# Row sums moved behind the transposes, one PSUM bank for all dispatches, an earlier v cast, and spare products in the tail of a linear-attention and soft-MoE kernel

## The chip, the cores and the metric

The kernel runs on one core of a Trainium2 chip. The metric is the device time of one launch in microseconds. Five engines work side by side, each with its own queue of instructions that it takes in order: PE multiplies matrices (its weight loads are shown as a separate row, PEld), DVE and ACT work elementwise and read the results out of PSUM, POOL works elementwise on SBUF, SP starts transfers. POOL starts transfers too. An engine waits for another one on a semaphore.

## The reference, cut to what matters

```
state = zeros(B, H, D, D)                       # B=4, H=8, S=768, D=48
for t in range(S):
    cur   = (u * k_t) outer v_t
    y_t   = r_t @ (state + cur)
    state = w[:, None] * state + k_t outer v_t
x = y as (B*S, H*D) = (3072, 384)

logits = x @ phi                                # (3072, 32): 8 experts, 4 slots each
d = softmax of logits over the 3072 rows        # dispatch
slot_out[e] = relu((d.T @ x)[e] @ w1[e]) @ w2[e]   # w1: 8 x 384 x 1024, w2: 8 x 1024 x 384
c = softmax of logits over the 32 slots         # combine
out = c @ slot_out
```

The kernel never subtracts a maximum. It keeps exp(logits) once, as `Le` (rows of x on the partitions) and transposed as `LexpT` (slots on the partitions, 3072 columns). The dispatch sum and its normaliser come from `Le`. The combine step needs for each of the 3072 rows the sum of exp(logits) over the slots: these **row sums** are products of columns of `LexpT` with a vector of ones.

## The kernel before, in words

**The loop.** The 8 heads are taken as 4 pairs, so there are 16 units (4 batches by 4 pairs), index `m` or `mu`. A unit has two halves of 384 time steps (`g` = 0 and 1, three chunks of 128 each), so the loop has 32 steps `i` and five steps of run-in; step `i` is even for the first half of a unit and odd for the second. k and r are scaled by powers of w on POOL (`scale`), transposed on PE (`t_pe`: k into bank T0 in even steps, r into bank T1 in odd ones) and copied out by ACT (`t_evac`, tiles `kT` and `rT`). In odd steps k is transposed back (`b_pe`, into T0) and copied out by DVE (`b_evac`, tile `kn`). `v_cast` turns v into bf16 on ACT (tile `v_bf`), `v_pe` spreads it over the partitions, `v_evac` copies it out. `a_pe` makes the scores in bank Ab, `mask_f` masks them on DVE (tile `AT`, line L303). `m_pe` and `z_evac` make the states (`Z`, `dv`), `y_pe` puts the result together, `y_evac` copies it to `x`. `prod_f` on DVE multiplies r, straight from bank T1, by k.

All instructions stand in the order in which the code is written; nothing reorders them. The code is written as a software pipeline: step `i` holds `a_pe(i+1)`, `y_pe(i)`, `v_pe(i+2)`, `m_pe(i+1)`, the transposes of unit `mu+2` and, at its end, `v_cast(mu+2)` in odd steps. `v_pe` of the very next step is the first to read that cast.

**The routing inside the loop.** While batch `b+1` is computed, `route(i, part)` does the expert routing of batch `b`, spread over the 8 steps `s` = 0 to 7: `xt_mm` transposes a chunk of x and ACT copies it out (`xT`); one step later `lg_mm` makes its logits; after three chunks ACT takes the exponential (`le_ev`). At `s` = 4 and `s` = 7 a finished half batch is dispatched: `disp` (twelve products, lines L421 and L425), `disp_ev` (DVE adds the result to `acc`), and `le_t` and `let_ev` (the transpose into `LexpT`). The dispatch at `s` = 4 writes the end of bank T1 (`ds_e`), the one at `s` = 7 the end of bank T0 (`ds_o`). Both stand ahead of the step's transposes. A wait is for a whole bank's tile: a dispatch that writes the end of T1 waits until `prod_f` has read the front of T1, and `b_pe`, which writes T0, waits until `acc` has been taken out of T0. ACT and DVE also read one bank's tile one after the other, in the order of the code.

**The weights.** w1 and w2 are loaded by transfers that POOL starts (`load_w`), converting to bf16 on the way. The table `W_AT` says after which loop step how many of the 16 are started; w2 goes into the buffers of batches 1 and 2.

**The tail.** After the loop the last two half batches (6 and 7) go through transposes, logits, exponential and dispatch. Then 24 row-sum products with 96 columns of weights each (L539, for the rows of the first six half batches), the dispatch of half batch 7, the sums `uns` on DVE, the w1 products (L565: 48 products of 512 columns, four of them side by side in the array), relu on ACT and DVE, eight transposes per group (L577), two copies of the transposed hidden layer (`hT`: DVE L580, ACT L582), the w2 products (L588), 24 row-sum products with 32 columns (L599, the remaining rows) ahead of the last expert's share of w2, and at last 24 products `LexpT` by `so` (L620), scaled by DVE and ACT and written out in eight transfers. The weights of all row sums and of L620 are every 24th column of `LexpT`.

`keep_warm` (L139) multiplies a tile of zeros; it stands only at the start of the kernel.

Of the kernel before, what the change touches and what calls it, by code (L numbers as in the profile page):

```python
# [9 lines left out]
def kernel(  # L10
# [26 lines left out]
    T = L * C  # L37
    P2 = 2 * D
    nN = Nn // C
    nG = B * G  # L40
    nU = B * nQ
# [10 lines left out]
    def O(ins):  # L52
        return tc.keep_in_program_order(ins)
# [35 lines left out]
    ds_e = T1[:, 768:1024].bitcast(f32)[:, 0:NA]  # L89
    ds_o = T0[:, 768:1024].bitcast(f32)[:, 0:NA]  # L90


    LexpT = cst.tile([128, Nn], bf, name="LexpT")
# [43 lines left out]
    def keep_warm(n, cols=512):  # L137
        for _ in range(n):
            O(pe.matmul(Yb[:, 0:cols], warm[:, 0:128], warm[:, 0:cols], start=True, stop=True))  # L139


    s_i = cst.tile([128, J], i32, name="s_i")
# [293 lines left out]
    def route(i, part):  # L436
        b, s = divmod(i - LAG, 2 * nQ)
        if not 0 <= b < B - 1 or i == nH - 1:
            return
        ne = 2 * b  # L440
        ch = [(ne, c) for c in range(L)] + [(ne + 1, c) for c in range(L)]
        done = {L + 1: ne, 2 * L + 1: ne + 1}.get(s)
        if part == 0:
            if done is not None:
                ds = ds_o if s % 2 else ds_e
                disp(done, ds)
                disp_ev(done, ds)
                le_t(done)
# [17 lines left out]
    for i in range(-5, nH):  # L466
        mu, odd = divmod(i, 2)
        if 0 <= i + 1 < nH:
            a_pe(i + 1)
            mask_f(i + 1)  # L470
        if odd == 0 and 0 <= mu + 1 < nU:
            prod_f(mu + 1)
        if i == nH - 1:
            for c, (bank, eng) in enumerate(((Vb[:].bitcast(bf)[:, 0:Dm], act), (T1[:, 0:Dm], dve), (xT_p, act))):
                xt_mm(nG - 2, c, bank)
                xt_ev(nG - 2, c, bank, eng)
        if 0 <= i < nH:
# [42 lines left out]
    disp(n0 - 1, ds_o)  # L520
# [12 lines left out]
    le_ev(n0 + 1, LG1)  # L533
    lp = Mb[:].bitcast(bf)[:, 0:T]
    le_t(n0, lp)
    let_ev(n0, lp)
    nP = (nG - 2) * T // nN
    for i in range(nN):
        O(pe.matmul(Rs[0:nP, i:i + 1], LexpT[:, i:nP * nN:nN], ones[:, 0:1],  # L539
                    start=(i == 0), stop=(i == nN - 1), skip_group_check=True))  # L540
    disp(n0 + 1, ds_o, False)


    for g in range(2):
        def half(t):
            return t[:, 0:nM * ES].rearrange("p (m j x) -> p m j x", m=nM, j=EG)[:, :, :, g * Spe:(g + 1) * Spe]
        O(dve.tensor_add(uns[:, :, g, :, g * Spe:(g + 1) * Spe], half(acc), half(ds_o)))
    le_t(n0 + 1)
    let_ev(n0 + 1)
    csr = cst.tile([128, 1], f32, name="csr")  # L550
    O(dve.scalar_tensor_tensor(out=csr[:], in0=acc[:, NA - 1:NA], scalar=1e-9, in1=ds_o[:, NA - 1:NA],
                               op0=ALU.add, op1=ALU.add))
    O(dve.reciprocal(csr[:], csr[:]))

# [6 lines left out]
    for g in range(2):  # L561
        for a in range(2):
            for mi in range(nM):
                for j in range(EG):
                    O(pe.matmul(hb[g][a][32 * j:32 * j + 32, 0:FH], uns[:, mi, g, j, :],  # L565
                                w1_all[:, g * EG + j, mi, a * FH:(a + 1) * FH],
                                start=(mi == 0), stop=(mi == nM - 1), skip_group_check=True))
            src = hb[g][a][:, 0:FH].rearrange("p (q y) -> p y q", y=nF)
            dst = h_sb[g][:, :, a * PH:(a + 1) * PH]
            if a == 0:  # L570
                O(act.activation(out=dst, in_=src, func=AF.Relu))
            else:
                O(dve.tensor_scalar(out=dst, in0=src, scalar1=0.0, scalar2=None, op0=ALU.max))
    for g in range(2):
        bank = (T0, T1)[g]
        for y in range(nF):
            O(pe.transpose(bank[:, y * C:(y + 1) * C], h_sb[g][:, y, :], ident[:]))  # L577
        dst = hT[g].rearrange("p y c -> p (y c)")
# [16 lines left out]
    for y in range(nF):  # L595
        for j in range(EG - 1):
            w2_mm(1, j, y)
    for i in range(nN):
        O(pe.matmul(Rs[nP:128, i:i + 1], LexpT[:, nP * nN + i:Nn:nN], ones[:, 0:1],  # L599
                    start=(i == 0), stop=(i == nN - 1), skip_group_check=True))  # L600
    rsr = cst.tile([128, nN], f32, name="rsr")
    O(dve.reciprocal(rsr[:], Rs))
    for y in range(nF):
# [53 lines left out]
```

## Time and profile before

| | |
|---|---|
| Median of 3 runs | 136.2 us (134.25, 136.2, 137.34) |
| Profiled execution | 134.71 us, of which the span from first to last instruction is 132.9 us |
| Granted clock of PE, mean | 0.951 |
| Busy: PE / PEld / DVE / ACT / POOL | 107.2 / 85.2 / 98.8 / 84.8 / 60.6 us |
| Weight transfers started by POOL | 12.59 MB, last bytes at about 105 us |
| Loop | first mask at 13.5 us, last at 96.3 us |
| Tail up to the first output transfer | 98 to 119 us |
| Output transfers | 119 us to the end |

A line of the timeline reads: start, time, engine, line, operation, destination and sources, shape, how many were merged, and in brackets how long the engine had stood idle before and what ended that. In a row of the windows the columns are the stretch, its length, busy time and number of instructions of PE, PEld, DVE, ACT and POOL, the granted clock of PE as a share of full speed, the share of the transfer engines that was busy, and GB/s. In the groups the last columns are total and mean time of one instruction. In the table of waits they are the total, how often, and the longest.

### The profile page before, as it was taken

The page shows a single profiled execution, that of the slowest core. Times are in us where ns is not written, and L with a number is a line of the kernel's source. Part 1 is how long each engine was busy: PE and PEld are TensorE (multiplying, and loading weights), DVE is VectorE, ACT ScalarE, POOL GpSimd, SP SyncE. Part 2 cuts the span into 40 slices and gives each one's busy share as a digit, 9 for nine tenths or more (in the row PEclk, how much of TensorE's full clock was granted, in tenths as well). Part 3 has the DMA queues.
Part 4 walks back from the last instruction along what each step waited for, and adds up shares of the span by engine and source line. Part 5 has one row for each costly group of instructions (what it writes and reads, how often), then busy time and mean ns, then how long its engine had stood idle before and what let it go on. Part 6 is the DMA issues. An engine that isn't in the chain of part 4 may idle for free.

```text
span 132.9 us, 4372 instructions
## 1 busy us (share of the span) xinstructions
PE 107.2 (81%) x1806; PEld 85.2 (64%) x1806; DVE 98.8 (74%) x197; ACT 84.8 (64%) x177; POOL 60.6 (46%) x72
## 2 busy tenths in 40 slices
PE   6497858989888979889888898987999998989100
PEld 1255737767667867777777687785889836975000
DVE  2999999999999995979997898999760123059500
ACT  3559857778578768977895978888672124049400
POOL 5979999984459636766493792100000000000000
PEclk9999999999999999999999999999999559999955
DMA  2999999999999999999999999999999700009995
GB/s 80 298 356 374 374 363 306 359 375 339 368 380 341 218 220 214 179 195 190 216 211 202 216 165 188 211 214 221 216 209 210 126 2 5 0 5 364 407 416 233
DMA packets 21093, 31.79 MB, mean 239 GB/s; under 512 B 1361, under 2 KB 18258, under 8 KB 21074
## 3 DMA queue, kind: packets, MB, share of 16 engines
q0 software_dynamic: 2656, 12.59, 47.9%
q1 hardware_dynamic: 18418, 18.93, 41.4%
q8 instruction: 14, 0.23, 0.6%
q14 instruction: 5, 0.04, 0.1%
HBM read 39.38 MB, written 4.72 MB: 332 GB/s over the span
## 4 chain that ended last, share of the span: by engine, by line
PE 43%; DVE 28%; issue 9%; ACT 9%; POOL 3%; DVEq 1%; POOLq 0%; ACTq 0%
DVE AT L303 6%; PE Vb L283 6%; DVE prod L256 5%; DVE Z L342 5%; DVE dv L344 5%; PE Ab L539 4%; PE T L234 3%; PE Yb L367 3%; PE Mb L324 3%; ACT rT L240 2%; PE Ab L298 2%; ACT kT L240 2%; DVE W L181 2%; PE T L246 2%; ACT v_bf L269 2%
## 5 line engine op out<-in xcount | busy, mean ns | idle before, releaser
L227 POOL TENSOR_TENSOR kr<-raw,W 128x576 bf16<-128x576 f32 x30 | 43.2, 1453 | 18.0 <-PE T L234 15.4
L303 DVE TENSOR_TENSOR AT<-Ab,mask_ut 128x768 bf16<-128x768 f32 x32 | 30.3, 948 | 2.0 <-PE Ab L298 2.0
L283 PEld LDWEIGHTS <-Q 128*128 128x128 bf16 x288 | 15.6, 97 | 10.4 <-issue 9.8
L283 PE MATMUL Vb<-v_bf,Q 128*128 128x96 bf16 x288 | 17.4, 205 | 5.4 <-ACT v_bf L269 4.6
L240 ACT COPY kT<-T 128x768 bf16<-128x768 bf16 x16 | 12.8, 800 | 7.4 <-PE T L234 6.5
L234 PE MATMUL T<-ident,kr 128*128 128x128 bf16 x192 | 16.4, 225 | 0.0
L240 ACT COPY rT<-T 128x768 bf16<-128x768 bf16 x16 | 12.8, 800 | 4.8 <-PE T L234 3.4
L374 ACT CAST x<-Yb 128x288 bf16<-128x288 f32 x32 | 13.1, 409 | 3.7 <-PE Yb L367 3.6
L256 DVE TENSOR_TENSOR prod<-T,kT 128x768 bf16<-128x768 bf16 x16 | 15.1, 946 | 0.0
L289 ACT CAST vn<-Vb 128x288 bf16<-128x288 f32 x32 | 13.0, 408 | 2.1 <-ACT x L374 1.4
L344 DVE TENSOR_TENSOR dv<-vn,Mb 128x288 bf16<-128x288 bf16 x32 | 14.2, 442 | 0.0
L234 PEld LDWEIGHTS <-kr 128*128 128x128 bf16 x192 | 12.3, 100 | 0.6 <-issue 0.6
L298 PE MATMUL Ab<-rT,kT 64*128 64x128 bf16 x192 | 10.9, 219 | 1.2 <-DVE AT L303 1.1
L324 PE MATMUL Mb<-vn,kn 128*128 128x96 bf16 (+2 forms) x80 | 11.2, 238 | 0.0
L342 DVE TENSOR_TENSOR Z<-Mb,bmask 128x192 bf16<-128x192 f32 x32 | 11.1, 346 | 0.0
L251 DVE COPY kn<-T 128x768 bf16<-128x768 bf16 x16 | 8.9, 554 | 2.3 <-PE T L246 2.0
L365 PE MATMUL Yb<-Z,rT 128*128 128x96 bf16 x80 | 9.4, 203 | 1.2 <-DVE Z L342 1.0
L354 PE MATMUL Yb<-vn,AT 128*128 128x48 bf16 x192 | 10.3, 185 | 0.0
L269 ACT CAST v_bf<-raw 128x576 bf16<-128x576 f32 x15 | 10.1, 676 | 0.0
L367 PE MATMUL Yb<-dv,ident 128*128 128x288 bf16 x32 | 9.1, 283 | 1.1
L398 ACT COPY xT<-Xb 128x384 bf16<-128x384 bf16 x19 | 9.2, 485 | 0.2 <-PE Xb L389 0.2
L354 PEld LDWEIGHTS <-AT 128*128 128x128 bf16 x192 | 7.0, 96 | 3.2
(140 smaller groups left out, 214.4 us busy)
## 6 DMA issues: line engine op xcount, KB each, us to landing
w_all<-in_moe_w_dram POOLq DMA_DIRECT2D x8, 768.0 KB, 9.1
raw<-in_moe_w_dram POOLq DMA_DIRECT2D x7, 768.0 KB, 15.2
out_dram<-raw SPq DMA_DIRECT2D x4, 768.0 KB, 5.9
raw<-in_k_dram SPq DMA_DIRECT2D x8, 288.0 KB, 6.6
raw<-in_r_dram SPq DMA_DIRECT2D x8, 288.0 KB, 6.1
raw<-in_v_dram SPq DMA_DIRECT2D x8, 288.0 KB, 6.4
raw<-in_k_dram SPq DMA_DIRECT2D x2, 1152.0 KB, 10.3
raw<-in_r_dram SPq DMA_DIRECT2D x2, 1152.0 KB, 9.9
```

What stands on the lines that cost most here:

```text
L227: O(eng.tensor_mul(kr[:, j].rearrange("p j (h s) -> p j h s", s=64)[:, :, :, 0:D], src, W[j][:, q].rearrange("p j (h d) -> p j h d", h=2)))
L234: O(pe.transpose(bank[:, x * C:(x + 1) * C], kr[:, j, x, :], ident[:]))
L240: O(act.copy(t[:].rearrange("p (s j) -> p s j", j=J), bank[:, 0:S].rearrange("p (j s) -> p s j", j=J)))
L256: O(dve.tensor_mul(pr[:].rearrange("p (s j) -> p s j", j=J), T1[:, 0:S].rearrange("p (j s) -> p s j", j=J), st["kT", m][:].rearrange("p (s ...
L283: O(pe.matmul(Vb[:, c * P2:(c + 1) * P2], Q3[:, o:o + C], vb[:, :, g, j, :], start=(j == 0), stop=(j == JV - 1)))
L298: O(pe.matmul(Ab[:, e, c * C:(c + 1) * C], kT[s, t], rT[s, t]))
L303: O(dve.tensor_mul(AT[:], Ab[:, :, 0:T].rearrange("p e (c t) -> p e c t", c=L), mask_ut[:, None, None, :].to_broadcast([128, 2, L, C])))
L324: O(pe.matmul(o, kn[:, g * L + c, :], vc, start=first, stop=True, skip_group_check=True))
L342: O(dve.tensor_mul(Z[:], Mb[:, 0:2 * P2].rearrange("p (c e) -> p c e", c=2), bmask[:, None, :].to_broadcast([128, 2, P2])))
L344: O(dve.tensor_mul(dv[:], st["v", i][:].rearrange("p c e d -> p (c e) d"), Mb[:, 288:288 + 2 * L, None].to_broadcast([128, L * 2, D])))
L354: O(pe.matmul(Yb[:, o:o + D], AT[:, e, c, :], vn[:, c, e, :], start=first, stop=False, skip_group_check=True))
L374: O(act.copy(st["x", n][:, :, q * P2:(q + 1) * P2], Yb[:, 0:L * P2].rearrange("p (c e) -> p c e", c=L)))
```

## The change

Four things are done at once.

1. The row sums are made in one go with 128 columns of weights each (24 products instead of 24 of 96 and 24 of 32). The first eight stand between the transposes of the two groups, the other sixteen where L599 stood. The copy of the second `hT` is halved between DVE and ACT.
2. Every dispatch in the loop writes the end of T1 (`ds_p`), and it stands behind the step's `t_pe` (`route(i, 1)`). The logits and the x transposes stay ahead of it (`route(i, 0)`); the copies of ACT stay at the end (`route(i, 2)`).
3. `v_cast` stands in even steps, one step earlier. `W_AT` starts some weight transfers one step earlier.
4. In the tail five products of 512 columns (`busy`, on a tile of w1, into the second half of Ab, never read) stand between the routing steps.

```
+    def busy(n):
+        keep_warm(n, Ab[:, 1, :], w1_all[:, 0, 0, :])
...
     le_ev(n0, LG0)
+    busy(1)
     for c, (bank, eng) in enumerate(...):
         xt_mm(n0 + 1, c, bank)
         xt_ev(n0 + 1, c, bank, eng)
-    disp(n0, ds_o, False)
+    busy(1)
+    disp(n0, ds_t, False)
+    busy(1)
     for c in range(L):
         lg_mm(n0 + 1, c, LG1)
     le_ev(n0 + 1, LG1)
+    busy(1)
...
-    for i in range(nN):
-        O(pe.matmul(Rs[0:nP, i:i + 1], LexpT[:, i:nP * nN:nN], ones[:, 0:1], ...))
-    disp(n0 + 1, ds_o, False)
+    disp(n0 + 1, ds_t, False)
+    busy(1)
...
+    def row_sums(a, z):
+        for i in range(a, z):
+            O(pe.matmul(Rs[:, i:i + 1], LexpT[:, i:Nn:nN], ones[:, 0:1], ...))
...
         if g == 0:
-            O(dve.tensor_copy(dst, bank[:]))
+            O(dve.tensor_copy(flat(hT[g]), bank[:]))
+            row_sums(0, 8)
         else:
-            O(act.copy(dst, bank[:]))
+            O(dve.tensor_copy(flat(hT[g])[:, 0:F // 2], bank[:, 0:F // 2]))
+            O(act.copy(flat(hT[g])[:, F // 2:F], bank[:, F // 2:F]))
...
-    W_AT = {13: 1, 14: 1, 15: 1, 17: 1, 18: 1, 20: 1, 21: 1, 23: 1, 24: 1, 26: 1, 27: 5}
+    W_AT = {13: 1, 14: 1, 15: 1, 16: 1, 18: 1, 19: 1, 21: 1, 22: 1, 23: 1, 25: 1, 26: 5}
...
         if 0 <= mu + 2 < nU:
             t_pe(mu + 2, odd)
+            route(i, 1)
             t_evac(mu + 2, odd)
...
-        if odd and 0 <= mu + 2 < nU:
+        else:
+            route(i, 1)
+        if odd == 0 and 0 <= mu + 2 < nU:
             v_cast(mu + 2)
-        route(i, 1)
+        route(i, 2)
```

**ACT, one unit with routing, before** (copies of k, of the x transpose, of x, v and r, the cast of v, the exponential):

```order
L240 COPY kT<-T_71 128x768
L398 COPY xT<-Xb 128x384
L374 CAST x<-Yb 128x3x96
L289 CAST vn<-Vb 128x288
L240 COPY rT<-T_72 128x768
L269 CAST v_bf<-raw_68 128x576
L404 ACTIVATE Le_167<-Xb 128x12x8
```

The same place in the changed kernel, whose lines are numbered one higher here:

```order
L241 COPY kT<-T_71 128x768
L270 CAST v_bf<-raw_68 128x576
L399 COPY xT<-Xb 128x384
L375 CAST x<-Yb 128x3x96
L290 CAST vn<-Vb 128x288
L241 COPY rT<-T_72 128x768
L405 ACTIVATE Le_167<-Xb 128x12x8
```

The cast has moved from behind the copy of r to behind the copy of k, and so ahead of the even step's copy `xT`.

**PE at the first dispatch of a batch (`s` = 4), before** (T_71 is bank T0, T_72 is bank T1):

```order
L421 LDWEIGHTS x
L421 MATMUL T_72<-Le_167,x 128x32
...
L425 MATMUL T_72<-ones,Le_167 128x1
...
L411 MATMUL Xb<-ident,Le_167 128x128
...
L382 MATMUL Xb<-phi_s,xT 128x32
...
L389 MATMUL Xb<-ident,x 128x128
...
L234 MATMUL T_71<-ident,kr_140 128x128
```

And in the changed kernel:

```order
L383 MATMUL Xb<-phi_s,xT 128x32
...
L390 MATMUL Xb<-ident,x 128x128
...
L235 MATMUL T_71<-ident,kr_140 128x128
...
L422 MATMUL T_72<-Le_167,x 128x32
...
L426 MATMUL T_72<-ones,Le_167 128x1
...
L412 MATMUL Xb<-ident,Le_167 128x128
```

The logits, the x transposes and the k transposes now stand ahead of the dispatch; the dispatch and the transpose of `Le` are the last thing ahead of the scores of the next step.

**PE in the tail, before** (the end of the logits of half batch 7, the first row sums, the dispatch of half batch 7):

```order
L382 MATMUL Yb<-phi_s,xT 128x32
...
L411 MATMUL Mb<-ident,Le_167 128x128
...
L539 LDWEIGHTS LexpT
L539 MATMUL Ab<-ones,LexpT 96x1
...
L421 MATMUL T_71<-Le_168,x 128x32
```

In the changed kernel:

```order
L383 MATMUL Yb<-phi_s,xT 128x32
...
L140 MATMUL Ab<-w_all 128x512
...
L412 MATMUL Mb<-ident,Le_167 128x128
...
L422 MATMUL T_71<-Le_168,x 128x32
...
L575 MATMUL Ab<-w_all,uns 32x512
...
L595 MATMUL T_71<-ident,W_152 128x128
...
L586 MATMUL Ab<-ones,LexpT 128x1
```

Between the logits and the dispatch one wide product stands in place of the row sums, whose first ones now come behind the transposes of the first group.

More of the change, by code (lines that the diff above doesn't have):

```diff
@@ L88 @@
     NA = nM * ES + 1
-    ds_e = T1[:, 768:1024].bitcast(f32)[:, 0:NA]
-    ds_o = T0[:, 768:1024].bitcast(f32)[:, 0:NA]
+    ds_p = T1[:, 768:1024].bitcast(f32)[:, 0:NA]
+    ds_t = T0[:, 768:1024].bitcast(f32)[:, 0:NA]
     LexpT = cst.tile([128, Nn], bf, name="LexpT")
@@ L135, in load_w, with keep_warm @@
                              in_=moe_w2[n - E].rearrange("(p y) d -> p y d", p=128)[:, y0:y1, :]))
-    def keep_warm(n, cols=512):
+    def keep_warm(n, bank=Yb, data=None):
+        data = warm if data is None else data
         for _ in range(n):
-            O(pe.matmul(Yb[:, 0:cols], warm[:, 0:128], warm[:, 0:cols], start=True, stop=True))
+            O(pe.matmul(bank[:, 0:512], data[:, 0:128], data[:, 0:512], start=True, stop=True))
     s_i = cst.tile([128, J], i32, name="s_i")
@@ L442, in route @@
         done = {L + 1: ne, 2 * L + 1: ne + 1}.get(s)
-        if part == 0:
[L444 to L448, printed above, removed]
+        if part == 1:
+            if done is not None:
+                disp(done, ds_p)
+                disp_ev(done, ds_p)
+                le_t(done)
+            return
+        if part == 0:
             if 1 <= s <= 2 * L:
@@ L519 @@
     Ab0, Rs = Ab[:, 0, :], Ab[:, 1, 0:nN]
-    disp(n0 - 1, ds_o)
+    def busy(n):
+        keep_warm(n, Ab[:, 1, :], w1_all[:, 0, 0, :])
+    disp(n0 - 1, ds_t)
     le_t(n0 - 1)
@@ L536 @@
     let_ev(n0, lp)
-    nP = (nG - 2) * T // nN
-    for i in range(nN):
-        O(pe.matmul(Rs[0:nP, i:i + 1], LexpT[:, i:nP * nN:nN], ones[:, 0:1],
-                    start=(i == 0), stop=(i == nN - 1), skip_group_check=True))
-    disp(n0 + 1, ds_o, False)
+    disp(n0 + 1, ds_t, False)
+    busy(1)
     for g in range(2):
@@ L546, in half @@
             return t[:, 0:nM * ES].rearrange("p (m j x) -> p m j x", m=nM, j=EG)[:, :, :, g * Spe:(g + 1) * Spe]
-        O(dve.tensor_add(uns[:, :, g, :, g * Spe:(g + 1) * Spe], half(acc), half(ds_o)))
+        O(dve.tensor_add(uns[:, :, g, :, g * Spe:(g + 1) * Spe], half(acc), half(ds_t)))
     le_t(n0 + 1)
@@ L550 @@
     csr = cst.tile([128, 1], f32, name="csr")
-    O(dve.scalar_tensor_tensor(out=csr[:], in0=acc[:, NA - 1:NA], scalar=1e-9, in1=ds_o[:, NA - 1:NA],
+    O(dve.scalar_tensor_tensor(out=csr[:], in0=acc[:, NA - 1:NA], scalar=1e-9, in1=ds_t[:, NA - 1:NA],
                                op0=ALU.add, op1=ALU.add))
@@ L573, with flat @@
                 O(dve.tensor_scalar(out=dst, in0=src, scalar1=0.0, scalar2=None, op0=ALU.max))
+    def row_sums(a, z):
+        for i in range(a, z):
+            O(pe.matmul(Rs[:, i:i + 1], LexpT[:, i:Nn:nN], ones[:, 0:1],
+                        start=(i == 0), stop=(i == nN - 1), skip_group_check=True))
+    def flat(t):
+        return t.rearrange("p y c -> p (y c)")
     for g in range(2):
@@ L597 @@
             w2_mm(1, j, y)
-    for i in range(nN):
-        O(pe.matmul(Rs[nP:128, i:i + 1], LexpT[:, nP * nN + i:Nn:nN], ones[:, 0:1],
-                    start=(i == 0), stop=(i == nN - 1), skip_group_check=True))
+    row_sums(8, nN)
     rsr = cst.tile([128, nN], f32, name="rsr")
```

1 line of the change is left out of this document (removed).

## The prediction

> **What bounds the kernel now.** I read the page first, then the windows of the tail, then the timeline of the tail and of a few loop steps.
>
> ```profile
> span 132.9 us, 4372 instructions
> PEclk9999999999999999999999999999999559999955
> ```
>
> The profiled execution took 134.71 us, 1.8 of it outside the span. No engine is full over the whole span, so the stages have to be read one by one. PE's granted clock is full except in two places; the first lies where the row sums and the w1 products are:
>
> ```profile
> 100.30:105.10 4.80, 4.80 (x27) 4.80 (x25) 0.00 (x0) 0.66 (x2) 0.00 (x0) 0.76 1.00 190
> 106.00:110.50 4.50, 4.50 (x49) 1.57 (x50) 0.91 (x3) 1.52 (x3) 0.00 (x0) 0.59 0.01 2
> 110.50:112.00 1.50, 1.05 (x20) 0.87 (x16) 1.29 (x2) 0.10 (x1) 0.00 (x0) 1.00 0.00 0
> ```
>
> For 4.8 us PE does nothing but load weights while DVE and POOL do nothing at all. The clock is halved in the middle of it (0.76 is a mean of 1 and 0.5) and comes back late in the w1 products (0.59). In the tail PE alone is the path:
>
> ```profile
> 99.51 0.39 PE L421 MATMUL T<-Le,x 128*128 128x32 bf16 x9
> ...
> 100.25 4.90 PEld L539 LDWEIGHTS <-LexpT 128*96 128x96 bf16 x24
> ...
> 105.10 0.41 PE L421 MATMUL T<-Le,x 128*128 128x32 bf16 x9
> ...
> 105.93 1.47 PE L565 MATMUL Ab<-w_all,uns 128*32 128x512 bf16 x12
> ...
> 109.71 0.82 PE L565 MATMUL Mb<-w_all,uns 128*32 128x512 bf16 x12
> ...
> 111.53 0.61 PE L577 MATMUL T<-ident,W 128*128 128x128 bf16 x8 [0.45 <-DVE W L573]
> ...
> 112.06 0.28 PE L588 MATMUL Xb<-raw,W 128*32 128x192 bf16 x4
> ...
> 114.58 1.54 PEld L599 LDWEIGHTS <-LexpT 128*32 128x32 bf16 x21
> ```
>
> After 119 us the output transfers bind (415 GB/s), so whatever the tail gains before them moves the end by as much:
>
> ```profile
> 122.00:125.00 3.00, 1.49 (x7) 0.61 (x5) 2.81 (x6) 2.35 (x5) 0.00 (x0) 1.00 1.02 415
> ```
>
> The loop is read from the starts of the mask on DVE, one in every step:
>
> ```profile
> 42.15 0.95 DVE L303 TENSOR_TENSOR AT<-Ab,mask_ut 128x768 bf16<-128x768 f32 x1
> 44.51 0.95 DVE L303 TENSOR_TENSOR AT<-Ab,mask_ut 128x768 bf16<-128x768 f32 x1
> 47.12 0.95 DVE L303 TENSOR_TENSOR AT<-Ab,mask_ut 128x768 bf16<-128x768 f32 x1
> 50.55 0.96 DVE L303 TENSOR_TENSOR AT<-Ab,mask_ut 128x768 bf16<-128x768 f32 x1 [0.79 <-PE Ab L298]
> 53.55 0.95 DVE L303 TENSOR_TENSOR AT<-Ab,mask_ut 128x768 bf16<-128x768 f32 x1
> 59.22 0.95 DVE L303 TENSOR_TENSOR AT<-Ab,mask_ut 128x768 bf16<-128x768 f32 x1
> ```
>
> A unit of two steps without dispatch takes 47.12 - 42.15 = 4.97 us. The unit with the first dispatch takes 6.43, that with the second 5.67: dispatching costs 1.46 and 0.70 us beyond an ordinary unit, and this comes twice.
>
> **The change part by part.** *Dispatch behind the transposes.*
>
> ```profile
> 48.99 0.41 PE L421 MATMUL T<-Le,x 128*128 128x32 bf16 x9 [0.52 <-DVE prod L256]
> ...
> 49.49 0.23 PE L382 MATMUL Xb<-phi_s,xT 128*128 128x32 bf16 x3
> ...
> 50.16 0.34 PE L298 MATMUL Ab<-rT,kT 64*128 64x128 bf16 x6
> ```
>
> At the first dispatch PE stands 0.52 us until prod has read T1, and only then come the dispatch, the logits and transposes (49.49 to 50.16, 0.67 us) and the scores, for which the mask waits 0.79. Put ahead of the dispatch, the 0.67 us are worked off while PE would wait. The scores, and so the mask at 50.55, come 0.67 earlier. The step after it took 3.00 us (50.55 to 53.55) against 2.61 in an ordinary unit (44.51 to 47.12), since ACT got k late and everything behind it slipped; that goes too: 0.67 + 0.38 = 1.05 us. prod still ends the wait, so some of the 1.46 stays.
>
> ```profile
> 57.35 0.50 PE L234 MATMUL T<-ident,kr 128*128 128x128 bf16 x6
> ...
> 58.21 0.49 PE L246 MATMUL T<-ident,kT 128*128 128x128 bf16 x6 [0.36 <-DVE acc L432]
> ```
>
> At the second dispatch `b_pe` waits 0.36 us until acc has left T0, behind PE's own transposes. With the dispatch in T1 nothing is in T0 to wait for. That saves the wait at least, and up to 0.52, since transposes queued behind others start before the last of those is through. DVE has acc ahead of the copy of kn either way, so I take 0.45. The copy of r now comes behind acc on the bank it shares; its readers are a unit away. The third dispatch has no k transposes to move, only half of the twelve products between 49.49 and 50.16: 0.3 us. Sum of the loop: 2 x (1.05 + 0.45) + 0.3 = **3.3 us**; at most it is 2 x 2.16 + 0.5 = 4.8, at worst a loss, as the next part shows.
>
> *The cast in even steps.*
>
> ```profile
> 41.97 0.68 ACT L269 CAST v_bf<-raw 128x576 bf16<-128x576 f32 x1
> 42.54 0.48 ACT L398 COPY xT<-Xb 128x384 bf16<-128x384 bf16 x1
> 42.70 0.54 PE L283 MATMUL Vb<-v_bf,Q 128*128 128x96 bf16 x9 [0.38 <-ACT v_bf L269]
> ...
> 43.28 0.22 PE L328 MATMUL Mb<-ucol,prod 128*128 128x2 bf16 x3
> ...
> 43.88 0.34 DVE L342 TENSOR_TENSOR Z<-Mb,bmask 128x192 bf16<-128x192 f32 x1
> ...
> 44.14 0.80 ACT L240 COPY kT<-T 128x768 bf16<-128x768 bf16 x1 [0.42 <-PE T L234]
> ...
> 44.83 0.48 ACT L398 COPY xT<-Xb 128x384 bf16<-128x384 bf16 x1
> ...
> 45.47 0.23 PE L382 MATMUL Xb<-phi_s,xT 128*128 128x32 bf16 x3
> ```
>
> PE's wait of 0.38 goes. I cost its gain at nothing: the next result that DVE takes from that step is Z at 43.88, right behind mask and prod, and the products for it end at 43.50. What it does cost is a place in ACT's queue: xT of the even step moves 0.57 us back (42.54 - 41.97 is the cast's share). The logits at 45.47 wait for xT, and behind them on PE stand the transposes, `b_pe` and the scores. Without the wait PE reaches the k transposes, and ACT the copy of k, 0.38 us earlier, so xT, which ended at 44.83 + 0.48 = 45.31, ends at 45.31 + 0.57 - 0.38 = 45.50, where its reader began at 45.47: zero, with nothing to spare. Bounds: if all of the 0.57 shows in the nine odd steps with logits, 5.1 us are lost; if all waits for the cast were on the path, the table of waits gives what there is to gain:
>
> ```profile
> PE Vb L283 <- ACT v_bf L269: 4.6, 12, 0.4
> ```
>
> On POOL the first cast now stands ahead of the second unit's k scaling:
>
> ```profile
> 10.90 1.19 POOL L267 CAST v_bf<-raw 128x576 bf16<-128x576 f32 x1
> ...
> 12.52 0.50 PE L234 MATMUL T<-ident,kr 128*128 128x128 bf16 x6
> ```
>
> The two only change places, so the scaling ends where the cast did, at 12.09, still ahead of its transposes at 12.52; cost zero, 0.5 if v lands later than I think. The weight transfers that POOL starts earlier were nearly back to back and ended here:
>
> ```profile
> 104.00:106.00 2.00, 0.50 0.63 112
> ```
>
> that is, at about 105.3 (0.63 of the window). They read and write no buffer in use and their issue delays a k scaling which PE needs steps later: zero. But their end does not move with the tail, and I come back to it below.
>
> *Row sums out of the critical place, wide products in.* 24 loads leave: -4.90 us. Five wide products come in. The w1 stage shows their price: 4.5 us at a mean clock of 0.59 are 2.66 us at full clock for twelve groups, 0.22 each, so +1.1. Two new short waits (a wide product for DVE's copy out of the same Ab, the dispatch for its exponential, which had the row sums to hide behind): +0.2, an estimate, with 0 and 0.6 as bounds. **-3.6 us.**
>
> *The clock.* The twelve groups took 109.71 + 0.82 - 105.93 = 4.60 us and need 2.7 at full clock. I take full clock, since PE now has dense work up to them: **-1.85 us**, bounds 0 and -1.9.
>
> *Row sums with 128 columns.*
>
> ```profile
> L539 PEld LDWEIGHTS <-LexpT 128*96 128x96 bf16 x24 | 4.9, 303 | 0.0
> ...
> L620 PEld LDWEIGHTS <-LexpT 128*128 128x128 bf16 x24 | 3.5, 149 | 2.2 <-issue 1.3 <-DVE so L606 0.7
> ...
> L599 PEld LDWEIGHTS <-LexpT 128*32 128x32 bf16 x24 | 1.7, 170 | 0.0
> ```
>
> One load with 96 columns lasts 303 ns and they follow each other every 204 (4.90 / 24); with 32 columns 170 ns, every 73 (1.54 / 21). In both about 98 ns are latency. L620 loads the very columns now wanted, 128 of them with the same stride, in 149 ns: 51 ns of occupancy. I take 60. Sixteen in place of L599: 24 x 0.073 - 16 x 0.060 = **-0.8 us**. The eight between the transposes (0.48) fit into the 0.45 us for which PE waits there for relu, plus 0.08 ahead of 112.06: zero. The upper bound is the rate of the 96-column row, 204 / 96 x 128 = 272 ns: the sixteen would take 4.35 us and the eight overrun by 1.6, so 5.0 us worse than my value. In the Trainium skill, page "TensorE: Matmul & The Clock Gate", section "LDWEIGHTS (loading the stationary operand)", a load takes its columns divided by 1.2, in ns: 107 here, by which, as an estimate, the sum would be 1.1 us smaller. The trace contradicts that rule for these strided columns at 96 (204 instead of 80).
>
> The halved copy of `hT` ends earlier than before, but its readers come 1.3 us after the first w2 product: zero.
>
> Sum: 3.3 + 3.6 + 1.85 + 0.8 = **9.55 us**. From 134.7 this gives 125.15; the median of the runs shown, 136.2, is 1.5 higher, and gives 126.65. I say **125.9**.
>
> **The rivals.** *The loop gains nothing* (15%): ACT's new order eats what the dispatch gives, by the margin that xT lacks. Then 125.9 + 3.3 = 129.2.
>
> *The clock falls anyway* (10%). The stretch ahead of w1 is made of small products and transposes with short waits. That costs 1.85, and the five wide products another 1.1: 128.9. For it: the fall at 100 to 105 came under a PE that was busy by the profile. Against it: the loop, made of the same products, has full clock in every slice. The same page of the Trainium skill, section "Part 4: PE-mode transpose", says that transposes do not count as activity for the clock gate, which speaks for this rival; here the clock stays full through 80 us with transposes in every step.
>
> *The 128-column loads go at the rate of the 96-column row* (6%): 125.9 + 5.0 = 130.9.
>
> *The weights land too late* (2%): they start behind L599, at 114.58 + 1.54 = 116.1; with 9.55 off that is 106.55, 1.2 us after 105.3. Each us of further gain or of late landing is then lost.
>
> *The cast was on the path* (6%): up to 4.6 more: 121.3.
>
> *Slower: ACT becomes what the loop waits for* (4%). Every unit grows by the cast that now stands ahead of xT, x and v: 16 x 0.57 = 9.1 us, and the dispatches gain nothing: 125.9 + 3.3 + 9.1 = 138.3. It outweighs the tail's 6.25 us from 0.39 us a unit on. Against it: ACT has idle time in each unit, 0.42 ahead of kT alone.
>
> **How the numbers follow.** My own case has 57%. The range leaves out the slower rival, the slow loads and the far end of the cast: 123.0 to 130.3. A measurement of this kernel can tell about 2%, 2.7 us: each case but the slower one lies below 133.5, and two rivals together would come near it, for which I keep 3%. Faster 0.93, same 0.03, slower 0.04.
>
> **What would show it.** Right: no slice below full clock until the output; units of about 5.4 and 5.2 us in place of 6.43 and 5.67; no wait of L283 for the cast; w1 products in 2.7 us, starting 6.9 us earlier; row-sum loads every 50 to 60 ns. Wrong: L382 waiting for xT in odd steps; a mask interval above 4.97 in ordinary units; PE waiting for a weight transfer in front of the last w2 products.

## The result and the profile after

The changed kernel took **126.37 us** in the median of four runs (125.57, 126.19, 126.54, 127.66) against 136.2; the ratio is 0.930, with an interval of 0.917 to 0.944. The ratios here and below leave out the slow runs of each kernel, those over 1.5% above its fastest, so they are not quotients of the medians. The forecast was 125.9, with 123.0 to 130.3 as its range. The profiled execution took 126.19 us where that of before took 134.71, so 8.52 us are to be found. First the page of the changed kernel:

```profile
span 124.4 us, 4333 instructions
PEclk9999996799999999999999999999999999999955
```

The two fives in the tail are gone; from the loop up to the output the clock is full. New is a fall at slices 7 and 8, in the run-in, to which I return. The masks of the changed kernel's timeline (DVE) show the loop:

```profile
42.28 0.95 DVE L304 TENSOR_TENSOR AT<-Ab,mask_ut 128x768 bf16<-128x768 f32 x1
44.63 0.95 DVE L304 TENSOR_TENSOR AT<-Ab,mask_ut 128x768 bf16<-128x768 f32 x1
47.26 0.95 DVE L304 TENSOR_TENSOR AT<-Ab,mask_ut 128x768 bf16<-128x768 f32 x1
50.08 0.96 DVE L304 TENSOR_TENSOR AT<-Ab,mask_ut 128x768 bf16<-128x768 f32 x1 [0.21 <-PE Ab L299]
52.74 0.95 DVE L304 TENSOR_TENSOR AT<-Ab,mask_ut 128x768 bf16<-128x768 f32 x1
57.95 0.95 DVE L304 TENSOR_TENSOR AT<-Ab,mask_ut 128x768 bf16<-128x768 f32 x1
...
93.39 0.95 DVE L304 TENSOR_TENSOR AT<-Ab,mask_ut 128x768 bf16<-128x768 f32 x1
```

The unit with the first dispatch now takes 52.74 - 47.26 = 5.48 us (6.43 before), that with the second 5.21 (5.67); an ordinary one still 4.98. The mask's own wait of 0.79 behind the first dispatch is down to 0.21. The tail, from PE's timeline and its weight loads:

```profile
96.99 0.38 PE L140 MATMUL Ab<-w_all 128*128 128x512 bf16 x1 [0.18 <-DVE xT L397]
...
99.26 0.83 PE L575 MATMUL Ab<-w_all,uns 128*32 128x512 bf16 x12
...
101.22 0.82 PE L575 MATMUL Mb<-w_all,uns 128*32 128x512 bf16 x12
...
103.56 0.28 PE L607 MATMUL Xb<-raw,W 128*32 128x192 bf16 x4
...
109.54 0.49 PE L637 MATMUL T<-so,LexpT 128*128 128x384 bf16 x2 [0.51 <-ACT so L624]
```

```profile
102.37 0.64 PEld L586 LDWEIGHTS <-LexpT 128*128 128x128 bf16 x8
...
106.32 1.20 PEld L586 LDWEIGHTS <-LexpT 128*128 128x128 bf16 x16 [0.16 <-issue]
```

L140 is a wide product, L575 are the w1 products (L565 before), L607 those of w2, L637 those of the output, L586 the row sums. Set against the same points of before (mask 47.12 and 96.32, w1 105.93, w2 112.06, output 118.05, end 132.9):

| stage | before | after | change | forecast |
|---|---|---|---|---|
| start to the mask of the 14th step | 47.12 | 47.26 | +0.14 | 0 |
| to the last mask | 49.20 | 46.13 | -3.07 | -3.3 |
| to the first w1 product | 9.61 | 5.87 | -3.74 | -3.6 |
| to the first w2 product | 6.13 | 4.30 | -1.83 | -1.85 |
| to the first output product | 5.99 | 5.98 | -0.01 | -0.8 |
| to the end | 14.85 | 14.86 | +0.01 | 0 |

Three terms came out within 0.25 us of what was worked out. One, the row sums with 128 columns, gave nothing.

### The profile page after: what moved, and what is told of

Read it like the earlier page. It is cut to its first block, busy times and chain, and to the rows that moved or that the text cites. A ratio compares the mean times of both kernels' runs of the same rounds, so it can differ in the third digit from the quotient of the medians.

```text
span 124.4 us, 4333 instructions
## 1 busy us (share of the span) xinstructions
PE 102.1 (82%) x1787; PEld 81.4 (65%) x1787; DVE 98.4 (79%) x198; ACT 84.0 (68%) x177; POOL 60.9 (49%) x72
## 4 chain that ended last, share of the span: by engine, by line
PE 36%; DVE 35%; issue 11%; DMA 5%; SPq 3%; POOL 2%; ACT 1%; DVEq 1%; POOLq 0%
DVE prod L257 11%; DVE AT L304 8%; DVE dv L345 6%; DVE Z L343 5%; DMA raw<-in_r_dram 5%; PE Vb L284 5%; PE Yb L368 3%; PE Mb L325 3%; PE T L235 2%; PE T L422 2%; PE T L247 2%; SPq L111 2%; PE Xb L607 2%; DVE raw L639 2%; PE Vb L607 2%
## 5 line engine op out<-in xcount | busy, mean ns | idle before, releaser
L366 PE MATMUL Yb<-Z,rT 128*128 128x96 bf16 x80 | 10.5, 205 | 3.3 <-DVE Z L343 3.3
```

## The experiments

**The dispatch alone, and the cast alone.** The first kernel is the one of before with the new place and bank of the dispatch and nothing else:

```
-            if done is not None:          # in part 0, ahead of logits and transposes
-                ds = ds_o if s % 2 else ds_e
-                disp(done, ds)
...
+        if part == 1:                     # called behind t_pe; ds_p is the end of T1
+            if done is not None:
+                disp(done, ds_p)
...
```

> The kernel before with the order of the dispatch alone: dispatch in T1 behind the transposes, nothing else changed (the v cast stays in odd steps, the tail is the old one). The prediction's theory (dispatch 3.3 us, cast nothing): the units with the first and second dispatch take about 5.4 and 5.2 us in place of 6.43 and 5.67, the last mask comes 3.0 to 3.3 us earlier, and the time falls by the same, to about 133 (ratio 0.976). Rival (the cast's place is what lets the dispatch gain, since PE otherwise meets its 0.4 us wait for the cast as the next thing that is late): less than half of that, 1 to 1.5 us, and the waits for the cast stand there with a longer mean than 0.4 us.

It took 132.9 us (131.43 to 133.94), a ratio of 0.982 (0.975 to 0.989). The loop from the 14th mask to the last took 46.51 us, so 2.69 of the 3.07 come from the dispatch. (The 14th mask itself came 1.64 us later here than before, at 48.76, 1.06 of it ahead of the first mask; a clock that fell in the run-in lies in the rest.) The second kernel is the changed one with the cast put back:

```
-        if odd == 0 and 0 <= mu + 2 < nU:
+        if odd and 0 <= mu + 2 < nU:
             v_cast(mu + 2)
```

> The changed kernel with the v cast put back into odd steps; all else stays changed. Theory (cast at nothing): the time of the changed kernel, 126.4 within 0.5, with PE's wait for the cast back in the table of waits and no later mask. Rival A (cast needed by the new dispatch order): the dispatch units grow by 0.3 to 1 us each, 127.5 to 129. Rival B (the cast's wait was on the path in every unit): up to 4.6 us more, 131.

It took 127.9 us (127.52 to 128.52), a ratio of 0.951 (0.944 to 0.958). That is 1.5 us above the changed kernel by the medians, on another chip, but the loop explains only 0.38 of it: from the 14th mask to the last it took 46.51 us, as in the first kernel. Another 0.73 us lie between the first mask and the 14th, where this execution too had a fall of the clock. Most of them can be placed: from the 6th mask to the 7th the three profiled executions with the cast in odd steps took 3.27 or 3.28 us and the eleven others 2.73 to 2.79. In that interval DVE casts phi, here and then in the changed kernel:

```profile
30.32 1.00 DVE L511 CAST phi_s<-phi_f 128x32 bf16<-128x32 f32 x3
```

```profile
29.92 0.46 DVE L511 CAST phi_s<-phi_f 128x32 bf16<-128x32 f32 x3
```

In all fourteen the last of these three casts ends 0.20 to 0.21 us after the scaling that POOL does beside it, and that scaling ends 3.15 us after the 6th mask with the cast of v in odd steps, 2.6 to 2.7 with it in even ones. That DVE is held up by POOL there is likely, but not shown. So the cast is worth 0.38 us in the loop and about 0.5 in the run-in, not nothing. Where the 0.38 sits is seen in the dispatch alone, at ACT and then at PE behind the second dispatch:

```profile
58.88 0.80 ACT L240 COPY rT<-T 128x768 bf16<-128x768 bf16 x1 [0.99 <-DVE acc L432]
59.57 0.67 ACT L269 CAST v_bf<-raw 128x576 bf16<-128x576 f32 x1
```

```profile
60.30 0.54 PE L283 MATMUL Vb<-v_bf,Q 128*128 128x96 bf16 x9 [0.69 <-ACT v_bf L269]
```

With the dispatch in T1, ACT's copy of r waits 0.99 us until DVE has taken `acc` out of the same bank; the cast is queued behind that copy, and PE waits 0.69 us for the cast in place of about 0.4. The unit behind the second dispatch then takes 5.16 us against 4.97, twice. In the changed kernel the cast is done in the even step ahead, and nothing is late. This is the first experiment's rival, in kind but not in size: it took 0.38 us and not half of the gain.

**Are the wide products needed?** All five calls are taken out:

```
-    busy(1)            # five times in the tail
```

> The changed kernel without the five wide products in the tail. The prediction's terms: their own 1.1 us go; if they are what keeps the clock, the twelve groups of w1 take 4.6 us again in place of 2.7, so 0.8 us slower in all, 127.2. Rival A (the row sums alone had let the clock fall, and PE is dense without wide products): clock full, 1.1 us faster, 125.3. Rival B (the wide products stand where PE would wait anyway, and the clock stays): less than 0.4 us either way. The time from the last mask to the start of w1 (5.87 now) and the span of the w1 products tell them apart.

It took 125.46 us (124.83 to 127.07), a ratio of 0.931 (0.923 to 0.938), which is not to be told from the changed kernel's. The stages tell more. The last mask came at 92.75:

```profile
92.80:97.90 5.10, 4.65 (x105) 4.00 (x104) 2.69 (x10) 3.67 (x11) 0.00 (x0) 1.00 1.03 213
97.90:100.60 2.70, 2.70 (x49) 1.20 (x49) 0.96 (x4) 1.40 (x3) 0.00 (x0) 1.00 1.06 205
```

The windows show full clock ahead of w1 and in it. From the last mask to w1 it took 97.89 - 92.75 = 5.14 us, 0.73 less than with the wide products; from w1 to w2 4.30, as with them. So here they cost 0.73 us and keep nothing warm that would cool without them. With row sums and wide products both away the stage is 4.47 us shorter than before, not 4.90: the row sums had covered 0.43 us of waits.

**What lets the clock fall.** Two kernels put loads of 128 columns back at the old place of the row sums, without wide products and without the later row sums; one has 24, the other goes through them three times:

```
+    for x in range(3):                    # second kernel only
+        for i in range(nN):
+            O(pe.matmul(Rs[:, i:i + 1], LexpT[:, i % 18:18 * 128:18], ones[:, 0:1], ...))
     disp(n0 + 1, ds_t, False)
```

> The changed kernel without wide products and with 24 loads of 128 columns (stride 18, out of the part of LexpT that is written by then) and their one-column products at the old place of the row sums, before the dispatch of the last group; no row sums later. The row sums come out of other columns than the reference's, so only times count. Without row sums there, and without wide products, the last mask to the start of w1 took 5.14 us and w1 ran at full clock (4.30 us to the start of w2). Theory A (load rate by width alone): 24 x 0.075 = 1.8 us more, 6.9 us; the clock stays, since 1.8 us is too short a stretch of one-column products. Theory B (the place makes the rate): 24 x 0.2 = 4.9 us more, 10 us, and w1 to w2 again about 6 us with the clock halved. Between: 6.9 us, but the clock falls, w1 to w2 above 5 us; then it is the one-column products as such that let it fall.

> As the kernel with 24 loads of 128 columns at the old place of the row sums and no wide products, but with the 24 gone through three times (the sums come out threefold, out of other columns). 24 loads took 1.57 us there and the clock stayed full; 72 take about 4.7, as long as the 24 loads of 96 columns took in the kernel before (4.9). Theory (the length of the stretch of one-column products lets the clock fall): half clock from inside or just behind the stretch, the w1 products above 3 us in place of 2.7, start of w1 to start of w2 above 5 us in place of 4.30. Rival (the slow 96-column loads as such, or chance): full clock, 4.30 us. Either way the last mask to w1 grows from 6.27 by 48 x 0.065 = 3.1 us.

The first took 125.05 us in one run, the second 129.39. The loads of each, and the clock in the windows of the second:

```profile
97.42 1.57 PEld L547 LDWEIGHTS <-LexpT 128*128 128x128 bf16 x24
```

```profile
97.81 4.55 PEld L548 LDWEIGHTS <-LexpT 128*128 128x128 bf16 x72
```

```profile
99.00:101.00 2.00, 2.00 (x35) 2.00 (x35) 0.00 (x0) 0.00 (x0) 0.00 (x0) 1.00 1.08 208
101.00:103.00 2.00, 2.00 (x39) 1.84 (x37) 0.13 (x2) 0.00 (x0) 0.00 (x0) 0.68 0.77 138
103.00:105.00 2.00, 1.98 (x22) 0.77 (x24) 0.42 (x4) 0.78 (x2) 0.00 (x0) 0.50 0.12 21
```

24 loads in 1.57 us left the clock full, and w1 to w2 took 4.30 us. 72 loads in 4.55 us brought it to half, and w1 to w2 took 108.41 - 103.13 = 5.28. The kernel before had 24 loads there too, of 96 columns, and its clock fell within their 4.90 us. So the length of the stretch in which PE makes only one-column products decides here, not the width or the number of the loads. The Trainium skill, page "TensorE: Matmul & The Clock Gate", section "Part 1: The HAM clock gate (the "warmup" mystery)", speaks of a free-running activity window of about 3.4 us; 1.57 and 4.55 us lie on its two sides, so these runs agree with it, if PE counts as idle there although its rows read busy. It is not the whole account: in the run-in, below, the clock fell behind a wait of only 1.41 to 1.63 us. In the first of the two, last mask to w1 grew by 1.13 us only, since part of the loads stood where PE would have waited.

**Where the 0.8 us of the row sums went.** One product over the first 128-column block replaces all 24:

```
-            row_sums(0, 8)
-    row_sums(8, nN)
+    O(pe.matmul(Rs, LexpT[:, 0:Nn:nN], ones[:, 0:nN], start=True, stop=True, ...))
```

> The changed kernel with one product in place of the 24 row sums: the first block of columns is summed into all 24 columns at once, so 23 of the 24 sums are left out. It stands where the sixteen stood; nothing stands between the transposes. Theory (each 128-column load costs the 75 ns that the trace of the changed kernel shows, and the sixteen lie bare on the path): w2 start to the first output product falls from 5.98 us by 15 x 0.075 = 1.1, and up to 0.3 comes between the transposes: 1.1 to 1.4 us faster, 125.1. Rival (the last w2 products would wait there for something else, weights or the copy of hT, whatever stands ahead of them): no gain, 126.4, and a wait of PE at that place.

It took 125.77 us (125.31 to 127.07), a ratio of 0.936 (0.927 to 0.946). From w2 to the output it took 108.75 - 103.81 = 4.94 us, 1.04 less, which is 69 ns for each of fifteen loads. Between the transposes nothing was gained: w1 to w2 took 4.30 us, and PE's wait for relu was back with 0.44. The eight loads there cost nothing, as the forecast had it. (From the first output product to the end this execution, the slowest of its four, took 16.55 us in place of 14.86: products and issues came as in the changed kernel, but the last few bytes landed late. Only the stages ahead of that are compared.) What remains dear is a single load. Its timeline on PE, and behind it the same place in a kernel told of below that has no row sum there:

```profile
106.38 0.26 PE L606 MATMUL Vb<-raw,W 128*32 128x192 bf16 x3
106.57 0.24 PE L616 MATMUL Ab<-ones,LexpT 128*128 128x24 bf16 x1
106.74 0.26 PE L606 MATMUL Xb<-raw,W 128*32 128x192 bf16 x1
```

```profile
104.42 0.26 PE L602 MATMUL Vb<-raw,W 128*32 128x192 bf16 x3
104.51 0.28 PE L602 MATMUL Xb<-raw,W 128*32 128x192 bf16 x4
...
104.87 0.25 PE L602 MATMUL Xb<-raw,W 128*32 128x192 bf16 x1
```

A w2 product fills 32 of the array's columns, and rows marked x3 or x4 are products side by side, one row every 0.08 us. The load of 128 columns breaks this: 0.36 us from one row to the next, 0.28 more than usual, and the last expert's products, four rows of which ran beside the others (104.51 to 104.75), now all stand alone, 4 x 0.083 = 0.33. Together 0.6: without any row sum the stage takes 106.53 - 102.19 = 4.34 us, with one load 4.94, with sixteen 5.98. The 24 narrow loads of before had cost 5.99 - 4.34 = 1.65 us, as much as the sixteen wide ones. In the timeline of before they, 32 columns wide too, had begun beside w2 products:

```profile
114.38 0.26 PE L588 MATMUL Xb<-raw,W 128*32 128x192 bf16 x3
114.40 0.23 PE L599 MATMUL Ab<-ones,LexpT 128*32 128x1 bf16 x1
114.47 0.26 PE L588 MATMUL Vb<-raw,W 128*32 128x192 bf16 x3
```


**The slow rate of 96 columns.** The sixteen loads are cut to 96 columns, in their new place, so that a quarter of these sums is left out:

```
+    nP = 96
+    for i in range(8, nN):
+        O(pe.matmul(Rs[0:nP, i:i + 1], LexpT[:, i:nP * nN:nN], ones[:, 0:1], ...))
```

> The changed kernel with the sixteen row-sum loads, at their new place behind the w2 products, cut from 128 to 96 columns of the same stride; one product over the first block of columns stands between the transposes in place of the eight. Row sums of the last 32 rows and most of the first eight are left out. Theory A (the 204 ns belong to a 96-column load wherever it stands, as the clock does not matter to it): the sixteen take 16 x 0.204 = 3.3 us in place of 1.2, and the time from the start of w2 to the first output product grows from 5.98 to about 8.0. Theory B (the 204 ns belonged to the place before w1): 16 x 0.075 or less, 5.9 us. Prediction's bound for 128 columns, 272 ns, would be dead already by the trace of the changed kernel (75 ns).

In one run it took 129.81 us, and the stage 113.17 - 105.09 = 8.08:

```profile
107.85 3.30 PEld L619 LDWEIGHTS <-LexpT 128*96 128x96 bf16 x16 [0.16 <-issue]
```

206 ns for a load with 96 columns at full clock, 204 in the kernel before, 75 with 128 columns in the same place. The rate belongs to the width: fewer columns, and almost three times as long. The Trainium skill, page "TensorE: Matmul & The Clock Gate", section "Weight-path perf modes — Fast Weight Load (FWL) and DoubleRow", says that the fast load is on when the number of weights is 128 and the type is not FP32. The runs agree that 128 is the fast case; the prediction had weighed another section of that page and overlooked this one, which speaks for the change.

**The weight transfers.** The old table of steps is put back into the changed kernel:

```
-    W_AT = {13: 1, 14: 1, 15: 1, 16: 1, 18: 1, 19: 1, 21: 1, 22: 1, 23: 1, 25: 1, 26: 5}
+    W_AT = {13: 1, 14: 1, 15: 1, 17: 1, 18: 1, 20: 1, 21: 1, 23: 1, 24: 1, 26: 1, 27: 5}
```

> The changed kernel with the weight transfers issued at the steps of the kernel before. The prediction's theory (zero): they still land ahead of the last w2 products at 107.5, by about 103 to 105, and no wait of PE for a weight appears: 126.4, tail from last mask to first output transfer as now (17.2 us). Rival (the earlier issue is part of the gain): the last part lands after 107.5, PE waits for it ahead of the last w2 products, 0.5 to 2 us more.

One run took 127.41 us; its loop starts 1.2 us later (14th mask at 48.48), and its stages are the changed kernel's: 5.88, 4.30, 5.98. The windows show the transfers end at about 104.3, 3.8 us behind the start of w1; in the changed kernel that distance was 3.1. The last w2 products start at 108.77 and no weight is waited for. In the tail the table is worth nothing here.

**The row sums into waits.** The sixteen leave the w2 stage, and the wide products go. First eight behind the third output product and eight behind the eleventh:

```
+            if i in (2, 10):
+                row_sums(i + 6, i + 14)
+                O(dve.reciprocal(rs[(i + 6) // 8][:], Rs[:, i + 6:i + 14]))
```

> The changed kernel without wide products, with the sixteen row sums moved out of the w2 stage into the output stage: eight behind the third output product, eight behind the eleventh, each with its own reciprocal; the eight between the transposes stay. Theory (wide products 0.73 us and not needed for the clock; sixteen loads 1.04 to 1.3 us bare on the path; the output stage is bound by its transfers and hides both): last mask to first output transfer falls from 17.2 to about 15.2 us, and the time to 124.4 (ratio to the kernel before 0.915). Rival (the output stage has no room, its evictions wait for the reciprocals, whose reads share a bank with the sums): 0.5 to 1.5 us come back there, first output transfer to end above 13.85 us, 125 to 126.

It took 124.82 us (123.74 to 126.9), a ratio of 0.919 (0.909 to 0.928). The last mask to the first output transfer took 14.79 us in place of 17.16, even less than expected, but from the first output product to the end it took 15.47 in place of 14.86:

```profile
110.05 0.65 PE L581 MATMUL Ab<-ones,LexpT 128*128 128x1 bf16 x8 [1.00 <-ACT raw L638]
```

The sums lie in the second half of tile Ab, whose first half is one of the seven output buffers; output 9 had just been put there, so PE waited until ACT had read it, and by then had no products ahead for DVE and ACT. This is the rival's case, at its lower price. The next kernel puts eight behind the last w2 products, where PE waits for `so`, and eight right ahead of output 16, which waits for that same reader:

```
         w2_mm(1, EG - 1, y)
+    row_sums(8, 16)
...
+            if i == 16:
+                row_sums(16, nN)
```

> The changed kernel without wide products; row sums 0 to 7 between the transposes as now, 8 to 15 behind the last w2 products, where PE waits 0.66 us for so, 16 to 23 right ahead of output product 16, which itself writes the other half of the tile that holds the sums and so waits for the same reader. Theory (the second eight behind output product 10 stalled because they share the tile with output 9, which drained PE's lead over the evictions; 1.0 us): w2 start to first output product 4.4 us, first output product to the end 14.9 as in the changed kernel in place of 15.5, so last mask to end about 28.7 us and the time 123.9 (1.8% below the changed kernel). Rival (the eight do not fit into the wait and the second eight starve the evictions): 0.3 to 0.6 us come back, 124.5.

It took 124.0 us (123.09 to 125.33), a ratio of 0.920 (0.913 to 0.927), beside 0.919 for the kernel ahead of it; the medians differ by 0.8 us on two chips, so by the times alone it is not shown to be the better of the two. From w2 to the output it took 108.63 - 104.28 = 4.35 us and from there 14.87 to the end, as expected. (Its twin below gives 4.35 as well, and 15.12 to the end: there the issue of the first output transfers, which comes ahead of the last eight sums, took 0.3 us longer.)

**The clock in the run-in.** Its twin has four wide products ahead of the third step's scores:

```
+        if i == 1:
+            keep_warm(4)
```

> The same as the kernel with the row sums in gaps, and four wide products of 512 columns on PE ahead of the third step's scores in the run-in, where PE waits 0.6 to 1.6 us for the mask (16.3 to 17.95 us in the changed kernel). Theory (the half clock at 19 to 23 us, seen in some executions and not in others, follows the 2 us in which PE is busy for only 0.4; it costs about 1 us where it comes): no half clock in the run-in, the median 0.5 us below its twin and its runs closer together. Rival (the half clock comes from elsewhere, or the run-in is bound by DVE and the fall costs nothing): the same time as its twin, or up to 0.4 us slower by the four products.

It ran with the changed kernel itself on the same chip:

> The changed kernel itself, so that the two versions are compared with it on one chip. Expected 126.4 by both theories; the half clock in the run-in (about 1 us) comes in some of its executions and not in others if it is a matter of chance, and in all or none if the order of the cast in the run-in decides it.

With them the kernel took **123.39 us** (123.13 to 124.67), a ratio of 0.918 (0.913 to 0.924); the changed kernel took 125.60 (125.33 to 127.37), 0.935 (0.929 to 0.941). All six runs of the one lie below all six of the other, by 1.8% in the medians: this version beats both kernels. Of the run-in the profiles show this. In the changed kernel:

```profile
17.95 0.34 PE L299 MATMUL Ab<-rT,kT 64*128 64x128 bf16 x6 [1.62 <-DVE AT L304]
```

```profile
16.00:18.00 2.00, 0.38 (x8) 0.21 (x7) 2.00 (x3) 0.94 (x3) 2.00 (x2) 1.00 1.12 366
18.00:20.00 2.00, 1.40 (x24) 1.06 (x25) 2.00 (x4) 1.85 (x5) 2.00 (x3) 0.93 1.08 364
20.00:22.00 2.00, 2.00 (x23) 1.80 (x20) 1.19 (x4) 0.99 (x3) 2.00 (x2) 0.50 1.11 368
```

PE waits 1.62 us for the mask, and two microseconds later has half a clock. Of ten profiled executions with a wait of 1.41 to 1.63 us there, nine had the fall behind it, the kernel with the sums in the output had not; the kernel with the cast put back (1.39) had its fall earlier, at 13 to 16 us; in the kernel before (1.06) and without wide products (0.64) there was none. With the four products there was none either, in one execution. The fall costs about 1.1 us: from the first mask to the 14th it took 34.27 us in the repeated changed kernel and 33.12 with the sums in the output. That the four products prevent it is likely but not shown: the intervals of the two twins overlap, and 0.6 us lie between their medians, as expected, in six runs each.

## Why the prediction was right, point by point

- **Dispatch behind the transposes** (2 x 1.5 + 0.3 = 3.3): right, 3.07. The first dispatch gave 0.95 (said 1.05), the second 0.46 (0.45), the third 0.27 (0.3). But 0.38 of it needs the earlier cast. The sentence that the copy of r "now comes behind acc on the bank it shares; its readers are a unit away" looked at the readers of r and not at the cast queued behind that copy on ACT.
- **The cast in even steps** (zero, nothing to spare for `xT`): right that `xT` is not late, off in the gain by 0.38 in the loop and about 0.5 in the run-in, where the sum had nothing. In the changed kernel, first on ACT, then on PE:

```profile
44.99 0.48 ACT L399 COPY xT<-Xb 128x384 bf16<-128x384 bf16 x1
```

```profile
45.60 0.23 PE L383 MATMUL Xb<-phi_s,xT 128*128 128x32 bf16 x3
```

  `xT` ends at 45.47 (said 45.50), and PE reads it at 45.60 without waiting; the whole step lies 0.13 later than before, so 0.13 us were to spare. The slower rival, ACT as the bound, had no place from which to start.
- **Row sums out, wide products in** (-3.6): right at -3.74 with parts that made up for each other. The wide products cost 0.73 and not 1.1, the removal gave 4.47 and not 4.70.
- **The clock** (-1.85): right, -1.83, but not thanks to the wide products. The long stretch of one-column products had let it fall, and that it went was enough. The rival "the clock falls anyway" is refuted by the kernel without them.
- **Row sums with 128 columns** (24 x 0.073 - 16 x 0.060 = 0.8): this is the term that failed; it gave 0.01. The sixteen loads took 75 ns each in the trace (69 by the experiment) and not 60, which is 0.15 to 0.24; the 60 had come from taking 98 ns of latency off the 149 of L620. The larger part is a price that the sum did not have at all: 0.6 us for breaking the stream of w2 products that run side by side, a stream that the old narrow loads had partly shared. In all the new loads cost 1.64 us there in place of 0.96, and the old ones 1.65 in place of 1.75. The upper bound, the rate of the 96-column row, is refuted for 128 columns and confirmed for 96.
- **Weights, halved `hT`, eight loads between the transposes** (zero): the weights and the eight loads were shown to cost nothing; the halving was not tried by itself, but PE has no wait in front of the products that read that copy, which ends at 104.79.
- **From 134.71** the sum gave 125.15 and the profiled execution took 126.19. The difference is 0.8 for the row sums, 0.23 for the loop and 0.14 for the run-in, less 0.14 in the stage ahead of w1. The 0.14 of the run-in is a sum itself: from the first mask to the 14th it took 33.6 us before, 33.1 to 33.2 in the changed versions without a fall and 34.1 in this execution, so the earlier cast gave 0.4 to 0.5 and the fall took 0.9, and the first mask came 0.31 earlier.
- **That the median came so close** is in part luck. The forecast stood between 125.15, counted from the profiled execution, and 126.65, counted from the median. The profiled executions differ by 8.52 us and the medians by 9.83, and the 9.55 of the sum lies between; the 0.8 us that the row sums did not give is lost in that spread and shows only in the stages.
- **The signs.** The units (5.48 and 5.21), the missing wait for the cast and the w1 products (2.78 us, starting 6.67 earlier) came as said. Two did not: the clock fell in the run-in, and the row-sum loads came every 75 to 80 ns.

## What to carry to other kernels

Before an operation is put into a stream that runs in strips side by side, price the break and not only the operation: one load of 128 columns cost 0.6 us there, and fifteen more 1.04. Look for waits in which work is free, and then for who shares its buffer: eight row sums cost nothing between transposes and nothing measurable behind the last w2 products, but 0.6 us in the output where they shared a tile with a result not yet read. When a product is put in to keep the clock, try the kernel without it as well.

## What the runs showed of the hardware that was not expected

A weight load of 96 columns is slower than one of 128 with the same stride: 204 to 206 ns against 75 to 80, and 206 against 75 in one and the same place at full clock (63 to 65 ns with 128 columns at a stride of 18). A stretch of one-column products that PE's rows show as fully busy lets the clock fall when it lasts 4.55 us, and not when it lasts 1.57. A wait of 1.41 to 1.63 us in the run-in was followed by half a clock in nine of ten executions and not in the tenth, so a single profile with or without such a fall, about 1.1 us here, says little of a change elsewhere. In all fourteen profiled executions the last of the three casts of phi on DVE ended 0.20 to 0.21 us behind the scaling that ran on POOL beside it, early or late.
